# Blocks 2 to 5 of a fused state-space and feed-forward kernel: transposing DMAs, two pairs per feed-forward matmul, tokens on partitions

## The chip, the cores and the metric

The kernel runs on one core of a Trainium2 chip. The time is device microseconds of one execution, and the kernel is judged by the median of its runs. A profile is one further execution, with its own time; its span runs from the first to the last instruction.

## The reference

A state-space layer over 4 batches, 8 heads, 768 tokens, head size 32 and state size 16, then a bilinear feed-forward over the 3072 tokens x 256 features.

```
for c in range(nc):                       # chunks of 32 tokens
    cum = np.cumsum(la, axis=-1)          # la = log(a) of the chunk
    L = np.exp(cum[:, :, :, None] - cum[:, :, None, :]) * causal
    M = np.einsum('bhin,bhjn->bhij', Cc, Bc) * L
    y_intra = np.einsum('bhij,bhjd->bhid', M, xc)
    y_inter = np.einsum('bhin,bhnd->bhid', Cc, state) * np.exp(cum)[:, :, :, None]
    y[:, :, sl] = y_intra + y_inter
    Bx = np.einsum('bhjn,bhjd->bhjnd', Bc, xc) * decay_from_j[:, :, :, None, None]
    state = decay_full[:, :, None, None] * state + np.sum(Bx, axis=2)
x = attn_out.transpose(0, 2, 1, 3).reshape(B * S, H * D)
return (x @ w_a) * (x @ w_b) @ w_out      # w_a, w_b: 256 x 1536, w_out: 1536 x 256
```

## The kernel before

The sequence is cut in 6 blocks of 128 tokens. A *pair* is one block of two batches, so there are 12 pairs; pair p is block p // 2. The decay inside a block is folded into B and C: `scan` makes running products of a, `factors_mm` spreads them to the tokens on TensorE, and `scale_bc` multiplies B and C by the factors (fB, fC) on GpSimd, so that the scores only need a causal mask.

For each pair: six loads (`load1`, L122) bring B, C and x of the two batches, batch bt on partitions 64 bt to 64 bt + 63, two neighbouring tokens on each partition, so that a run in memory is two tokens of a head (128 B for B and C, 256 B for x). `transposes` (L267) turns B and C on TensorE into the PSUM tile SC0; ScalarE evacuates B twice, each time with every second head zeroed, and C once (L274, L275). `scores` (L288) is 32 matmuls on 32 x 64 tiles of the array, into the four PSUM banks SC0 and SC1. `mask` (L321) multiplies each bank by the causal mask on VectorE, or through a ScalarE copy on GpSimd (L319). `pv` then adds the state product (L364), the product of the masked scores with x (L330) and, with `ds_mm` (L347), the sums for the next state; ScalarE writes the result as X2T (L378). `state_sums` (L405, VectorE) and `state_spread` (L412 and L419, GpSimd) make the next block's state as a full 128-column block-diagonal tile per batch.

The feed-forward of a pair has 256 token columns. A *unit* (`unit`, six per pair) is four matmuls for x @ w_a (L432, aps), four for x @ w_b (bps), one ScalarE copy of aps to asb (L444) and one VectorE product hk = bps x asb (L451). `out_half` is 12 matmuls with w_out for 128 tokens (L464), a ScalarE evacuation (L479) and a store (L481). All of these share four PSUM banks in turn (pool `psf`).

The order on every engine is written out by hand. From pair 3 on a loop issues: scores of p, scaling of pair p + 1 on GpSimd, loads of pair p + 2 on the SP queue, masks mixed with units of pair p - 1, output of p - 2, `pv(p)`, the transposes of p + 1. Stores and loads stand on the SP queue in this order too. Weights are loaded and cast by GpSimd's DMA queue, in halves for w_a and w_b and thirds for w_out; `warmup` matmuls run in the first 13 us.

## Time and profile before

| what | value |
|---|---|
| three runs | 131.08, 132.76, 135.22 us (median 132.76) |
| profiled execution | 130.84 us, span 129.1 us |
| TensorE busy | 122.9 us (95%), granted clock 1.0 |
| VectorE, ScalarE, GpSimd busy | 86.5, 75.2, 54.5 us |
| chain that ended last | TensorE 88% |
| feed-forward matmuls | 288 each of aps, bps and ops |
| DMA | 12.22 MB, 43333 packets |

In the rows, a line number is that of the kernel; "out<-in" names tiles; "x32" is a count; for a group, "busy, mean ns" and the idle time before it follow the bar. PEld is TensorE's weight load, which overlaps its matmuls. A matmul's length includes its way through the array, so the cost of one in a row of them is the difference of starts. SPq rows are DMA issues of the SP queue.

### The profile page before, as it was taken

The page shows a single profiled execution, that of the slowest core. Times are in us where ns is not written, and L with a number is a line of the kernel's source. Part 1 is how long each engine was busy: PE and PEld are TensorE (multiplying, and loading weights), DVE is VectorE, ACT ScalarE, POOL GpSimd, SP SyncE. Part 2 cuts the span into 40 slices and gives each one's busy share as a digit, 9 for nine tenths or more (in the row PEclk, how much of TensorE's full clock was granted, in tenths as well). Part 3 has the DMA queues.
Part 4 walks back from the last instruction along what each step waited for, and adds up shares of the span by engine and source line. Part 5 has one row for each costly group of instructions (what it writes and reads, how often), then busy time and mean ns, then how long its engine had stood idle before and what let it go on. Part 6 is the DMA issues. An engine that isn't in the chain of part 4 may idle for free.

```text
span 129.1 us, 4719 instructions
## 1 busy us (share of the span) xinstructions
PE 122.9 (95%) x1944; PEld 101.7 (79%) x1944; DVE 86.5 (67%) x162; ACT 75.2 (58%) x155; POOL 54.5 (42%) x77
## 2 busy tenths in 40 slices
PE   6999989998999999999999999999999999999990
PEld 2254778886888888888888888898888888888880
DVE  1695498693874975956957938948939929734441
ACT  3164946956566476476576576575486485455520
POOL 6777596587809309219129039047056000000000
PEclk9999999999999999999999999999999999999999
DMA  3999999956463542623623434515510110110112
GB/s 68 179 138 227 163 221 186 189 105 122 111 115 115 84 124 64 122 63 74 116 61 86 84 85 96 107 46 106 122 39 28 45 41 5 41 41 5 41 41 81
DMA packets 43333, 12.22 MB, mean 95 GB/s; under 512 B 37552, under 2 KB 43216, under 8 KB 43312
## 3 DMA queue, kind: packets, MB, share of 16 engines
q1 hardware_dynamic: 38256, 8.84, 32.6%
q0 software_dynamic: 2800, 2.63, 13.1%
q10 hardware_dynamic: 2256, 0.46, 1.8%
q8 instruction: 15, 0.25, 0.8%
q14 instruction: 6, 0.05, 0.1%
HBM read 11.13 MB, written 3.15 MB: 111 GB/s over the span
## 4 chain that ended last, share of the span: by engine, by line
PE 88%; DMA 3%; POOL 2%; DVE 2%; ACT 1%; issue 1%; SPq 0%
PE aps L432 25%; PE ops L464 24%; PE bps L432 23%; PE SC L288 3%; PE SC L330 3%; PE SC L267 3%; DMA bn<-in_B_dram 3%; PE SC L364 2%; PE tc L195 1%; DVE t L321 1%; PE fps L219 1%; PE SC L347 1%; POOL xn L122 1%; PE py L330 1%; POOL Wa L136 1%; ACT bt L274 1%
## 5 line engine op out<-in xcount | busy, mean ns | idle before, releaser
L451 DVE TENSOR_TENSOR hk<-bps,asb 128x512 f16<-128x512 f32 x72 | 49.3, 688 | 24.4 <-ACT asb L444 21.9
L444 ACT COPY asb<-aps 128x512 f32<-128x512 f32 x72 | 42.0, 587 | 18.3 <-PE aps L432 16.8
L432 PE MATMUL aps<-X2T,Wa 128*128 128x256 f16 x288 | 43.3, 275 | 0.0
L432 PE MATMUL bps<-X2T,Wb 128*128 128x256 f16 x288 | 42.9, 273 | 0.0
L464 PE MATMUL ops<-Wo,hk 128*128 128x256 f16 x288 | 35.2, 273 | 0.0
L321 DVE TENSOR_TENSOR t<-SC,causal 128x512 f16<-128x512 f32 x45 | 29.5, 682 | 2.8 <-PE SC L288 1.9
L432 PEld LDWEIGHTS <-Wa 128*128 128x128 f16 x288 | 27.5, 99 | 4.4 <-DVE Pr L200 0.3
L432 PEld LDWEIGHTS <-Wb 128*128 128x128 f16 x288 | 28.1, 98 | 3.3
L464 PEld LDWEIGHTS <-hk 128*128 128x128 f16 x288 | 27.7, 98 | 3.1
L412 POOL TENSOR_TENSOR sbd<-U,maskbd 128x512 f16<-128x512 f32 x10 | 11.6, 1160 | 35.7 <-DVE U L405 35.7
L479 ACT ACTIVATE osb<-ops 128x256 f32<-128x256 f32 x23 | 8.7, 386 | 15.7 <-PE ops L464 15.7
L243 POOL TENSOR_SCALAR x<-xn 128x512 f16<-128x512 f32 x9 | 13.4, 1491 | 0.9 <-DMA xn<-in_x_dram 0.2
L378 ACT ACTIVATE X2T<-SC 128x512 f16<-128x512 f32 x11 | 6.6, 597 | 8.3 <-PE SC L347 7.4
L274 ACT ACTIVATE bt<-SC,ch 128x256 f16<-128x256 f16 x22 | 9.2, 472 | 0.4 <-PE SC L267 0.3
L405 DVE SCALAR_TENSOR_TENSOR U<-SC,G,gU 128x64 f32<-128x64 f32 x16 | 3.8, 279 | 5.4 <-ACT X2T L378 5.4
L249 POOL TENSOR_TENSOR bm<-bn,fB 128x256 f16<-128x256 f32 x11 | 6.9, 626 | 0.8 <-DMA bn<-in_B_dram 0.8
L249 POOL TENSOR_TENSOR cm<-cn,fC 128x256 f16<-128x256 f32 x10 | 6.2, 623 | 1.3 <-DMA cn<-in_C_dram 1.3
L288 PEld LDWEIGHTS <-bt 32*64 32x64 f16 x384 | 3.6, 108 | 3.5 <-issue 2.2
L288 PE MATMUL SC<-ct,bt 32*64 32x128 f16 x384 | 5.4, 227 | 0.7 <-ACT ct L275 0.6
L195 PE MATMUL SC<-warm 128*128 128x512 f16 x10 | 4.8, 629 | 1.2 <-DVE warm L159 1.2
L330 PEld LDWEIGHTS <-x 64*32 64x32 f16 x384 | 3.1, 91 | 3.2 <-issue 1.1
L330 PE MATMUL SC<-t,x 64*32 64x128 f16 x352 | 4.6, 218 | 0.7 <-DVE t L321 0.7
(62 smaller groups left out, 73.1 us busy)
## 6 DMA issues: line engine op xcount, KB each, us to landing
out_dram<-osb SPq DMA_DIRECT2D x23, 128.0 KB, 1.7
xn<-in_x_dram SPq DMA_DIRECT2D x21, 128.0 KB, 3.2
bn<-in_B_dram SPq DMA_DIRECT2D x24, 64.0 KB, 3.2
cn<-in_C_dram SPq DMA_DIRECT2D x21, 64.0 KB, 2.9
Wa<-in_moe_w_a_dram POOLq DMA_DIRECT2D x2, 384.0 KB, 5.9
Wb<-in_moe_w_b_dram POOLq DMA_DIRECT2D x2, 384.0 KB, 7.4
Wo<-in_moe_w_out_dram POOLq DMA_DIRECT2D x3, 256.0 KB, 7.4
xn<-in_x_dram POOLq DMA_DIRECT2D x2, 128.0 KB, 7.2
```

Source lines behind the costliest of these rows:

```text
L243: eng.tensor_scalar(xo, xi, XS, None, ALU.mult)
L249: eng.tensor_tensor(out=m_, in0=pair_in[p][which].rearrange("p h r n -> p r h n"), in1=f[:, blk, :, bp].unsqueeze(3).broadcast_to((128, 2, ...
L274: nc.scalar.activation(out=o_, in_=TB, func=AF.Copy, scale=par[:, e : e + 1])
L288: nc.tensor.matmul(SC[m][64 * bt : 64 * bt + 64, c0 : c0 + Q], BT[rows, e, r, bt], CT[rows, bt], start=True, stop=True, skip_group_check=True,
L321: nc.vector.tensor_tensor(out=o_, in0=i_, in1=c_, op=ALU.mult)
L330: nc.tensor.matmul(py[bt][32 * g : 32 * g + 32, u * Q : (u + 1) * Q], s["X16"][k, h, r, :], s["T1"][k, h, r, :], start=(first and u == 0 a ...
L412: nc.gpsimd.tensor_tensor(out=Sbd.rearrange("p t (m c) -> p t m c", m=4), in0=U32[:, p].unsqueeze(2).broadcast_to((128, 2, 4, 2 * D)), in1 ...
L432: nc.tensor.matmul(ps[:, kk * 2 * Q : (kk + 1) * 2 * Q], W[:, f, k * 128 : (k + 1) * 128], X2T[:, p, f].rearrange("p t q -> p (t q)"), sta ...
L444: nc.scalar.copy(asb, a_ps)
L451: nc.vector.tensor_tensor(out=s["hk"][:, 2 * k2 : 2 * k2 + 2, :].rearrange("p k q -> p (k q)"), in0=b_ps, in1=asb, op=ALU.mult)
L464: nc.tensor.matmul(o_ps[:, 0:d_model], hk[:, k, bt * Q : (bt + 1) * Q], Wo[:, k, :], start=(k == 0), stop=(k == NK - 1), skip_group_check= ...
L479: nc.scalar.activation(out=o_sb, in_=o_ps[:, 0:d_model], func=AF.Copy, scale=1.0 / (YS * YS))
```

## The change

From block 2 on (pairs 4 to 11, `P0 = 4`) the layout is another one. Each partition holds one token, and both batches lie side by side on it (`by_token`); B, C and x of a pair come in one load each, with runs of one token (64 B for B and C, 128 B for x). `scale_bc` writes C, and in two copies B, into a tile of six planes of 128 columns, four of them B with every second head zero; `turn` transposes the six planes with one DMA on the SP queue, in place of the transposes on TensorE and their evacuations. Scores become 16 matmuls of 32 x 128 tiles, the product with x 16 of 128 x 32 and the state sums 8; the state product is 8 matmuls of 32 x 64 with a state tile of 64 columns (`spair`), a fraction of the former spread. `outputs` does all this for the two pairs of a block together and writes XB, on whose 512 token columns `bunit` runs the feed-forward, two matmuls for each weight matrix and 128 rows of it; `bout` makes the output of 128 tokens. The four PSUM banks (ff0 to ff3) are taken in a written order (`BANKS`) and no longer in turn. w_out is loaded in two parts with three neighbouring rows on a partition, and the columns of w_a and w_b are read with a step of three to match.

Pairs 0 to 3 keep their layout. In the start, the first loads, warm-ups, scans and masks stand in another order, pair 0's C is cut over two queues, three loads of pair 1 and all of pair 2 go through GpSimd's queue, and C of pair 0 is scaled from PSUM. The written order after pair 2 is new; pair 0's stores stand ahead of pair 4's x on the SP queue.

```diff
+    Wa = [big.tile([128, 2, KC], f16, name=f"Wa{t}") for t in range(2)]
+    Wb = [big.tile([128, 2, KC], f16, name=f"Wb{t}") for t in range(2)]
...
+    X2T = big.tile([128, P0, 2, 2, Q], f16, name="X2T")
+    XB = big.tile([128, NBLK - P0 // NBP, 2, 2, NBP, Q], f16, name="XB")
...
+    planes = [big.tile([128, 6, H * N], f16, name=f"planes{t}") for t in range(2)]
+    causal_q = big.tile([128, Q], f16, name="causal_q")
...
+    hkb = ctx.enter_context(tc.tile_pool(name="hkb", bufs=2))
...
+    def bank(name):
+        return psf.tile([128, 512], f32, name=name, tag=f"ff{next(banks)}")
...
+    def by_token(t_):
+        return t_.rearrange("p h r n -> p (h r n)").rearrange("p (t h n) -> p t h n", t=2, h=H)
...
+    def load2(eng, p, which):
...
+        blk, bp = divmod(p, NBP)
+        return eng.dma_start(
+            by_token(pair_in[p][which]).rearrange("p t h n -> p (t h) n"),
+            (B, C, x)[which][2 * bp : 2 * bp + 2, :, blk * Q : (blk + 1) * Q, :].rearrange("t h q n -> q (t h) n"),
+        )
...
+    def load_wo(half):
+        nc.gpsimd.dma_start(
+            Wo[:, 6 * half : 6 * half + 6].rearrange("p (g kk) e -> p g (kk e)", kk=3),
+            moe_w_out.rearrange("(g p kk) e -> p g (kk e)", p=128, kk=3)[:, 2 * half : 2 * half + 2],
+        )
...
+    load1(nc.scalar, 0, 0, 1)
+    load1(nc.sync, 0, 0, 0)
     load1(nc.scalar, 0, 1, 1)
-    b0 = load1(nc.sync, 0, 0, 0)
-    load1(nc.scalar, 0, 1, 0)
-    load1(nc.sync, 0, 0, 1)
+    load1(nc.sync, 0, 1, 0, 0, 32)
+    nc.sync.dma_start(ch, ph_t.ap())
+    load1(nc.scalar, 0, 1, 0, 32, 32)
     nc.scalar.preload_act_table_set("natural_log_exp_and_others")
     load1(nc.scalar, 0, 2, 1)
     load1(nc.sync, 0, 2, 0)
-    load1(nc.scalar, 1, 1, 1)
     load1(nc.sync, 1, 0, 0)
-    load1(nc.sync, 1, 1, 0)
...
-    w0 = load_w(0)
-    tc.add_manual_dep(w0[0].ins, b0.ins.name, AFTER, reason="first inputs ahead of weights")
+    load1(nc.gpsimd, 1, 0, 1)
+    load1(nc.gpsimd, 1, 1, 0)
+    load1(nc.gpsimd, 1, 1, 1)
+    load_w(0)
     for bt in range(2):
         load1(nc.gpsimd, 1, 2, bt)
-    b2 = load1(nc.sync, 2, 0, 0)
-    tc.add_manual_dep(b2.ins, w0[0].ins.name, AFTER, reason="first weights ahead of pair 2")
-    load1(nc.sync, 2, 0, 1)
-    for w in (1, 2):
-        for bt in range(2):
-            load1(nc.sync, 2, w, bt)
...
+        raw = by_token(pair_in[p][which]) if p >= P0 else pair_in[p][which].rearrange("p h r n -> p r h n")
+        if p >= P0 and which:
+            eng.tensor_tensor(
+                out=planes[p % 2][:, 4:6].rearrange("p t (h n) -> p t h n", n=N),
+                in0=raw,
+                in1=f[:, blk, :, bp].unsqueeze(3).broadcast_to((128, 2, H, N)),
+                op=ALU.mult,
+            )
+            return
...
+        if p >= P0:
+            dst = planes[p % 2][:, 0:4].rearrange("p (t e) (m f n) -> p t e m f n", e=2, f=2, n=N)
+            for e in range(2):
+                eng.tensor_copy(dst[:, :, e, :, e], m_.rearrange("p t (m f) n -> p t m f n", f=2)[:, :, :, e])
...
+    def turn(p):
+        T_ = mid.tile([128, 6, 128], f16, name="turned", tag="turned")
+        nc.sync.dma_start(T_, planes[p % 2].rearrange("p a c -> p (a c)"), transpose=True)
+        st[p]["BT"] = T_[:, 0:4].rearrange("p (t e) k -> p e t k", e=2)
+        st[p]["CT"] = T_[:, 4:6]
...
-        for e in range(2):
+        st[p]["T1"] = mid.tile([128, H, 2, Q], f16, name="t1", tag="t1")
+        for e, bt, m in itertools.product(range(2), range(2), range(4)) if p >= P0 else ():
+            rows = slice(32 * m, 32 * m + 32)
+            c0 = (e * 2 + bt) * Q
+            nc.tensor.matmul(
+                SC[m][:, c0 : c0 + Q],
+                BT[rows, e, bt],
+                CT[rows, bt],
+                start=True,
+                stop=True,
+                skip_group_check=True,
+                tile_position=(32 * m, 0),
+            )
+        for e in range(2) if p < P0 else ():
...
-        for r in range(2):
+        for bt, g in itertools.product(range(2), range(4)) if p >= P0 else ():
+            c0 = 32 * (g ^ 2 * bt)
+            nc.tensor.matmul(
+                py[bt, u][c0 : c0 + 32],
+                by_token(s["X16"])[:, bt, u * 4 + g],
+                s["T1"][:, u * 4 + g, bt],
+                start=False,
+                stop=True,
+                skip_group_check=True,
+                tile_position=(0, c0),
+            )
...
+        for bt, m in itertools.product(range(2), range(4)) if p >= P0 else ():
+            nc.tensor.matmul(
+                s["DS"][bt][32 * m : 32 * m + 32, :],
+                s["bm"][:, bt, 2 * m : 2 * m + 2, :].rearrange("p h n -> p (h n)"),
+                by_token(s["X16"])[:, bt, 2 * m : 2 * m + 2].rearrange("p h d -> p (h d)"),
+                start=True,
+                stop=True,
+                skip_group_check=True,
+                tile_position=(0, 32 * m),
...
+    def outputs(blk):
+        pairs = range(blk * NBP, (blk + 1) * NBP)
+        SCt = (SC0, SC1)
+        cols = [slice(j * Q, (j + 1) * Q) for j in range(NBP)]
+        for j, p in enumerate(pairs):
+            s = st[p]
+            for m in range(4):
+                for bt in range(2):
+                    rows = slice(32 * m, 32 * m + 32)
+                    half = 64 * ((m + bt) % 2)
+                    nc.tensor.matmul(
+                        SCt[bt][half : half + 64, m // 2, cols[j]],
+                        s["Sbd"][rows, bt],
+                        s["CT"][rows, bt],
+                        start=(j == 0),
+                        stop=False,
+                        skip_group_check=True,
+                        tile_position=(32 * m, half),
+                    )
...
+        for j, p in enumerate(pairs):
+            py = {(bt, u): SCt[bt][:, u, cols[j]] for bt in range(2) for u in range(2)}
+            for u in range(2):
+                pv_u(p, u, py, False)
...
+            nc.scalar.activation(
+                out=XB[to, blk - P0 // NBP, :, bt].rearrange("p u j q -> p u (j q)"),
+                in_=SCt[bt][fr, :, 0 : NBP * Q],
+                func=AF.Copy,
+                scale=YS / XS,
...
+        else:
+            Sbd = mid.tile([128, 2, 2 * D], f16, name="spair", tag="spair")
+            nc.gpsimd.tensor_tensor(
+                out=Sbd.rearrange("p t (e d) -> p t e d", e=2),
+                in0=U32[:, p].rearrange("p t (e d) -> p t e d", e=2),
+                in1=par.unsqueeze(1).unsqueeze(3).broadcast_to((128, 2, 2, D)),
+                op=ALU.mult,
+            )
...
                     ps[:, kk * 2 * Q : (kk + 1) * 2 * Q],
-                    W[:, f, k * 128 : (k + 1) * 128],
-                    X2T[:, p, f].rearrange("p t q -> p (t q)"),
+                    W[k // 6][:, f, k % 6 // 3 * 384 : (k % 6 // 3 + 1) * 384].rearrange("p (c kk) -> p kk c", kk=3)[
+                        :, k % 3
+                    ],
+                    X2T[:, p, :, f],
...
+    def bunit(blk, k):
+        s = st.setdefault(("FF", blk), {})
+        if "hk" not in s:
+            s["hk"] = hkb.tile([128, NK, 2 * NBP * Q], f16, name="hkb", tag="hkb")
+        ps = []
+        for W in (Wa, Wb):
+            t_ = bank("aps" if W is Wa else "bps")
+            for f in range(2):
+                nc.tensor.matmul(
+                    t_,
+                    W[k // 6][:, f, k % 6 // 3 * 384 : (k % 6 // 3 + 1) * 384].rearrange("p (c kk) -> p kk c", kk=3)[
+                        :, k % 3
+                    ],
+                    XB[:, blk - P0 // NBP, f].rearrange("p t j q -> p (t j q)"),
+                    start=(f == 0),
+                    stop=(f == 1),
+                    skip_group_check=True,
+                )
+            ps.append(t_)
+        asb = evac_a(ps[0])
+        return lambda: nc.vector.tensor_tensor(out=s["hk"][:, k], in0=ps[1], in1=asb, op=ALU.mult)
...
+    def bout(blk, c, parts=1):
+        bt, j = divmod(c, NBP)
+        hk = st[("FF", blk)]["hk"]
+        rows = out[(2 * j + bt) * S + blk * Q :][0:Q]
+        w = d_model // parts
+        for part in range(parts):
+            o_ps = bank("ops")
...
     warmup(6, SC[3])
+    warmup(2, SC[3], 128)
     scan(0, 1)
     over_mid(0, 1)
     sel_over_mid(0, 1, nc.vector)
+    scan(1, 3)
     v = factors_mm(0, 1)
     nc.vector.reciprocal(flat(fB, 0, 1), v)
+    warmup(2, SC[3])
+    warmup(1, SC[3], 128)
+    scale_bc(0, 0, nc.vector)
+    scale_bc(0, 1, nc.vector, v.rearrange("p (r b h) -> p r b h", r=2, b=NBP)[:, :, 0])
+    tb, tcp = bank("tb"), bank("tc")
+    transposes(0, [tb, tcp], lambda: warmup(1, SC[3], 128))
     nc.scalar.copy(flat(fC, 0, 1), v)
...
+    warmup(5, tcp)
...
+    scan(4, 5)
+    w1 = load_w(1)
+    for bt in range(2):
+        load1(nc.gpsimd, 2, 0, bt)
+    warmup(1, tcp, 128)
...
+    sel_over_mid(1, NBLK, nc.vector)
+    warmup(2, tcp)
+    aps = [unit_mm(0, 0, Wa), unit_mm(0, 1, Wa)]
+    asb = [evac_a(aps[0])]
     scores(1)
+    mask(product(1, 3), by_pool=True)
+    aps.append(unit_mm(0, 2, Wa))
+    asb.append(evac_a(aps[1]))
+    asb.append(evac_a(aps[2]))
+    fps = bank("fps")
+    factors(1, 3, fps)
+    scale_x(1, nc.scalar)
+    for m in range(3):
+        mask(product(1, m))
+    bps = [unit_mm(0, k2, Wb) for k2 in range(3)]
+    for bt in range(2):
+        load1(nc.gpsimd, 2, 1, bt)
+    load_wo(0)
...
+    load_wo(1)
+    tiles(3)
+    for bt in range(2):
+        load1(nc.gpsimd, 2, 2, bt)
+    times(0, 0, bps[0], asb[0])
+    pv(1, DS=(0, SC[:2]), split=True)
+    ds_mm(0, 64, SC[:2])
+    for k2 in range(1, 3):
         times(0, k2, bps[k2], asb[k2])
-    pv(1, then=lambda: ds_mm(0, 320))
-    v = factors_mm(3, NBLK)
+    fb(1)
+    scale_bc(2, 0, nc.gpsimd)
+    scale_bc(2, 1, nc.gpsimd)
+    go((1, 0), (1, 1), (1, 2))
...
+    for t_ in planes:
...
+    b3 = [load1(nc.sync, 3, 0, bt) for bt in range(2)]
+    tc.add_manual_dep(b3[0].ins, w1[1].ins.name, AFTER, reason="weights ahead of pair 3's inputs")
+    for bt in range(2):
+        load1(nc.sync, 3, 1, bt)
+    loads_x(3, nc.sync)
+    loads_bc(4)
+    go((0, 3), (0, 4), (1, 3), (0, 5))
+    transposes(2, apart=True)
...
+    loads_bc(5)
     o = [bank("ops"), bank("ops")]
-    for bt in range(2):
-        out_mm(0, bt, o[bt], range(8))
+    out_mm(0, 0, o[0], range(6))
+    out_mm(0, 1, o[1], range(6))
+    out_mm(0, 0, o[0], range(6, NK))
+    stores = [out_store(0, 0, o[0])]
     pull(2)
-    pv(2)
-    state(2)
+    pv(2, split=True)
+    out_mm(0, 1, o[1], range(6, NK))
+    stores.append(out_store(0, 1, o[1]))
+    h = unit(2, 0, lambda: transposes(3, apart=True))
+    state_sums(2)
...
+    def prep(p, spread=()):
+        if p < NP:
+            scale_bc(p, 1, nc.gpsimd)
+            scale_bc(p, 0, nc.gpsimd)
+            turn(p)
...
+    scores(3)
+    prep(4, (2,))
+    for f in stores:
+        f()
+    loads_x(4, nc.sync)
+    loads_x(5)
+    prep(5)
+    tiles(6)
+    load2(nc.sync, 6, 1)
+    load2(nc.sync, 6, 0)
+    loads_bc(7)
+    mask(product(3, 0))
+    h()
+    for m in range(1, 4):
+        mask(product(3, m))
+    out_half(1, 0)
+    out_half(1, 1)
+    go((2, 2))
+    pull(3)
+    pv(3)
+    state_sums(3)
+    fb(3)
+    state_spread(3)
+    prep_x(4)
+    go((2, 3), (2, 4), (2, 5))
+    out_half(2, 0)
+    o_ps = bank("ops")
+    out_mm(2, 1, o_ps, range(6))
...
+    scores(4)
+    mask(product(4, 3), by_pool=True, by_token=True)
+    scale_x(5, nc.scalar)
+    prep(6)
+    masked(4, (0, 1))
+    out_mm(2, 1, o_ps, range(6, NK))
+    out_store(2, 1, o_ps)()
+    masked(4, (2,), *pu(3, 0))
+    go((3, 1))
+    scores(5)
+    mask(product(5, 3), by_pool=True, by_token=True)
+    mask(product(5, 2), by_pool=True, by_token=True)
+    loads_x(6, nc.sync)
+    prep(7)
+    loads_x(7, nc.sync)
+    loads_bc(8)
+    masked(5, (0, 1), *pu(3, 2, 3, 4, 5))
+    group(2)
+    out_half(3, 0)
+    out_half(3, 1)
...
+    stage(6, True, (4, 5))
+    loads_x(8)
+    prep_x(7)
+    masked(6, (0, 1))
+    masked(6, (2,), *bu(2, 0, 1, 2))
+    scale_x(6, nc.scalar)
+    bgo(2, 3, 4)
+    stage(7, True)
+    loads_bc(9)
+    prep(8)
+    prep(9)
+    loads_x(9, nc.sync)
+    loads_bc(10)
+    masked(7, (0, 1, 2), *bu(2, 5, 6, 7, 8, 9, 10, 11))
+    group(3)
+    bout(2, 0)
+    bout(2, 1)
+    stage(8, True, (6, 7))
+    prep_x(8)
+    prep_x(9)
+    prep(10)
+    loads_bc(11)
+    loads_x(10, nc.sync)
+    masked(8, (0, 1))
+    masked(8, (2,), *bu(3, 0, 1, 2, 3, 4, 5))
...
+    for blk in range(4, NBLK):
+        pB = blk * NBP + 1
+        stage(pB, False)
+        if blk > 4:
+            prep_x(pB)
+        loads_x(pB + 2, nc.sync)
+        prep(pB + 2)
+        masked(pB, (0, 1))
+        bout(blk - 2, 2)
+        masked(pB, (2, 3), *bu(blk - 1, 6, 7, 8, 9))
+        group(blk)
+        bout(blk - 2, 3)
+        bgo(blk - 1, 10, 11)
+        if blk + 1 < NBLK:
+            stage(pB + 1, False, (pB - 1, pB))
+            prep_x(pB + 1)
+            masked(pB + 1, (0, 1))
+            bout(blk - 1, 0)
+            masked(pB + 1, (2,))
+            bout(blk - 1, 1)
+            masked(pB + 1, (3,), *bu(blk, 0, 1, 2, 3, 4, 5))
+    last = NBLK - 1
+    bout(last - 1, 0)
+    bout(last - 1, 1)
+    bgo(last, *range(6))
+    bout(last - 1, 2)
+    bgo(last, *range(6, NK))
+    bout(last - 1, 3)
+    for c in range(3):
+        bout(last, c)
+    bout(last, 3, 2)
```

## The prediction

> **What bounds the kernel now.** I read the busy shares first, then the chain of waits that ended last, then the timeline of TensorE over one pair, and last the rows of the engines that the change loads more.
>
> ```profile
> PE 122.9 (95%) x1944; PEld 101.7 (79%) x1944; DVE 86.5 (67%) x162; ACT 75.2 (58%) x155; POOL 54.5 (42%) x77
> PE 88%; DMA 3%; POOL 2%; DVE 2%; ACT 1%; issue 1%; SPq 0%
> ```
>
> The first line gives the busy time of each engine, the second the shares of the chain. TensorE (PE) is both the busiest and 88% of the chain, so a microsecond taken off its stream is a microsecond off the span as long as nothing else comes forward. The windows show how near the others are in the steady part (busy us of PE, PEld, DVE, ACT, POOL, then granted clock, DMA share, GB/s):
>
> ```profile
> 60.00:70.00 10.00, 10.00 (x167) 8.69 (x168) 7.70 (x15) 5.93 (x13) 4.70 (x7) 1.00 0.42 89
> 70.00:80.00 10.00, 10.00 (x168) 8.70 (x166) 7.44 (x14) 6.42 (x13) 4.79 (x6) 1.00 0.39 84
> ```
>
> TensorE never idles there, VectorE (DVE) is at 0.75, the clock is full. The timeline of one pair (start, length, row) says what the period is made of:
>
> ```profile
> 59.56 0.43 PE L288 MATMUL SC<-ct,bt 32*64 32x128 f16 x32
> 59.92 0.61 PE L432 MATMUL aps<-X2T,Wa 128*128 128x256 f16 x4
> 60.37 0.60 PE L432 MATMUL bps<-X2T,Wb 128*128 128x256 f16 x4
> ...
> 62.55 1.47 PE L464 MATMUL ops<-Wo,hk 128*128 128x256 f16 x12
> 63.86 0.60 PE L432 MATMUL aps<-X2T,Wa 128*128 128x256 f16 x4
> ...
> 64.73 0.39 PE L364 MATMUL SC<-ct,sbd 128*128 128x128 f16 x4
> 65.05 0.42 PE L330 MATMUL SC<-t,x 64*32 64x128 f16 x32
> 65.30 0.32 PE L347 MATMUL SC<-x,bm 64*32 64x64 f16 x16
> 65.56 0.29 PE L267 MATMUL SC<-ident,bm 128*128 128x128 f16 x2
> 65.68 0.28 PE L267 MATMUL SC<-ident,cm 128*128 128x128 f16 x2
> 65.79 1.47 PE L464 MATMUL ops<-Wo,hk 128*128 128x256 f16 x12
> ...
> 68.94 0.43 PE L288 MATMUL SC<-ct,bt 32*64 32x128 f16 x32
> ```
>
> Differences of starts are what counts, since ends overlap. The period is 68.94 - 59.56 = 9.38 us. Twelve output matmuls take 63.86 - 62.55 = 1.31, so 0.1092 us each; 72 feed-forward matmuls make 7.86. The attention part is the rest, 1.52: state product 0.32 (64.73 to 65.05), intra product 0.25, state sums 0.26, transposes 0.23, scores about 0.45 with the turn into and out of their tiling. So the feed-forward is near a floor that the change can't lower much, and 1.5 us of each pair is open to it.
>
> **The change, part by part: feed-forward of blocks 2 to 5.** Two pairs share one 512-column matmul, so the 96 matmuls of a block (two pairs, W_a and W_b) become 48 over the same columns. Price of a 512-column matmul: at most 2 x 109.2 = 218.4 ns; at least the 256-column one plus 256 columns at the slope between two rows of the page. L364's four of 128 columns are 57 ns apart ((390 - 219)/3), L432's four of 256 are 109 apart, so 0.404 ns a column, 212 ns. With 24 per pair the gain is 0 to 0.15 us; I take 0.07. Output matmuls stay at 256 columns.
>
> **Attention matmuls of pairs 4 to 11.** Tokens lie 128 to a block on partitions, no longer even and odd in halves. Transposes leave TensorE: -0.23. Scores fall from 32 matmuls on eighths of the array to 16 on quarters: at least four at a time by the 57 ns row (0.23), at most as before (0.45); I take 0.33. Intra product, 32 to 16, four at a time: 0.23 to 0.25, I take 0.24. State sums, 16 to 8: half of 0.26. State product, 4 full matmuls to 8 on eighths: 8 at the scores' 14 ns is 0.11, at most 0.32; I take 0.13. Sum 0.83 against 1.52: 0.69 less, bounds 0.36 to 0.82 by the ends named. Eight pairs: 8 x (0.69 + 0.07) = 6.1 us.
>
> **ScalarE and GpSimd.** ScalarE loses the three evacuations of the transposes (2 x 472 + 455 ns a pair) and gains some mask copies; it goes from 0.6 busy to less. GpSimd loses two thirds of the state spread (1160 ns for 512 columns, now 128: by the 406 ns row of the same size), gains two small copies a pair (at most 433 ns by the maskbd row) and some masks at 1.16. It has half its time free in the windows, so I cost this at nothing; if the cover were gone, a pair's copies would be 0.9 us. Early it is fuller: 3.6 to 4.1 of each 5 us until 35. Six loads of pair 2 at 0.72 move there, 4.3 us. What is late then is the first turn (pair 4), needed some 9 us after pair 3's scores; by my list of GpSimd's queue it has about 4 us left.
>
> **Start and end.** Three of pair 1's loads go onto GpSimd's queue ahead of the weights (3 x 0.72), a wait of 0.83 for pair 0's B and the 0.77 issue of ch leave it: weights leave 0.6 later and land at about 11.5, the first use was at 12.37. Covered by 0.9 us. The new order of warm-ups, scans and masks, and C cut over two queues, I bound by ±1.5 us (idle of 0.43 and 0.67 us in the timeline near 14 and 16 could go; the first loads end the wait at 4.6 either way) and take -0.4. The last store splits in halves of 128 columns: 24 x 57 ns against 12 x 109, no difference; the tail after the last matmul (some 3.2 us) stays.
>
> **Loads, turns and the SP queue.** This is the part the old trace can't show. Issues on SP (min/median/max ns):
>
> ```profile
> L122 SPq DMA_DIRECT2D bn<-in_B_dram x24: 596/627/1582, 1.2 to 87.6; - x24
> L122 SPq DMA_DIRECT2D xn<-in_x_dram x21: 595/633/1931, 2.7 to 90.5; - x21
> L481 SPq DMA_DIRECT2D out_dram<-osb x23: 332/338/577, 31.6 to 126.4; - x23
> ```
>
> B and x cost the same though x is twice the bytes; both have 512 runs, the store 128. So an issue goes by runs: 0.338 + 0.75 ns for each run above 128. A whole-pair load of the new kind has 2048 runs: 1.78 us (at least 0.63 if it didn't go by runs, at most 4 x 0.63 = 2.5). Runs double, 6144 a pair. The engines' side:
>
> ```profile
> q1 hardware_dynamic: 38256, 8.84, 32.6%
> ```
>
> 32.6% of 16 engines over 129.1 us is 17.6 ns a packet, for pieces of 231 B on average. 6144 pieces of 64 and 128 B cost between half of that and all of it: 3.4 to 6.8 us of 16 engines per pair, under a period of 8.6. The Trainium skill (DMA: Bandwidth & Descriptors, Specifications) speaks against the change here: it puts the smallest transfer for full line rate at 512 B, and its section on small descriptors counts a fixed three cycles for each packet. By it a 128 B piece is 7 cycles and a 64 B piece 5, so halving the pieces would cost 10/7 of the former packet time, an estimate from that page of about 5 us a pair; inside my ends.
>
> A turn (six blocks of 128 x 128, 192 KB) has no row. If it went by 256-byte rows it would be 768 runs, 0.82 us of SP; if by 16-element runs, 6144, 4.85 us. I take 0.8, being nearest to x's runs in length. The same skill page (Latency and other measured facts) gives a transposing DMA 261 GB/s, an estimate of 0.75 us for 192 KB; nothing here shows it.
>
> Does SP keep up? It starts pair 3's six loads when the second weights have landed (12.17 + 7.4, 19.6), is through at 23.4, and then issues 22 whole loads, 8 turns, 10 stores before the last turn is out: 39.2 + 6.4 + 3.4 = 49.0, so 72.4, landed at 75.5. TensorE wants that turn for pair 11's scores, after which it has 108 x 0.109 + 18 x 0.87 + 24 x 0.057 + 0.6 = 29.4 us and the tail of 3.2: 32.6 before the end, at about 91. There is 15 us of room on average, less for the first turns (pairs 5 to 8), where SP's queue holds a turn behind up to four loads (7.1 us). A turn waits for GpSimd's planes, and stores and loads of later pairs queue behind it. I put 0.5 us of stalls on that.
>
> **VectorE.**
>
> ```profile
> L451 DVE TENSOR_TENSOR hk<-bps,asb 128x512 f16<-128x512 f32 x72 | 49.3, 688 | 24.4 <-ACT asb L444 21.9
> L321 DVE TENSOR_TENSOR t<-SC,causal 128x512 f16<-128x512 f32 x45 | 29.5, 682 | 2.8 <-PE SC L288 1.9
> ```
>
> A block asks 12 x 0.688 + 8 x 0.682 + 4 x 0.28 + 0.34 = 15.2 us of it, TensorE 2 x 8.6 = 17.2: 0.88 against 0.80 before. Ahead of a joint group 4 masks and 4 products (5.5 us) stand against 12 output matmuls and 4 units (4.8 us): up to 0.7 late, and TensorE then waits for a bank. I take 0.15 for each of four blocks, 0.6 in all; ends 0 and 2.8.
>
> **The sum.** Span 129.1 - 6.1 - 0.4 + 0.5 + 0.6 = 123.7. Around the span lay 130.84 - 129.1 = 1.74 us, so 125.4 against the profiled 130.84, a ratio of 0.959. The three runs were 131.08, 132.76 and 135.22; the profiled one is under the lowest. Scaled to the median it would be 127.2, to the lowest 125.7; I give 126.2.
>
> **Rivals.**
> First, more gain: attention at its lower ends (0.82 + 0.15 a pair, 7.8), start -1.5, no stalls: span 119.8, time 121.5. For it: VectorE's longest waits are for ScalarE, which gets lighter. Against: every end must hold at once.
>
> Second, VectorE takes the place: 0.6 lost in each of the eight pairs' stages (the 0.7 above is the worst of them), 4.8 less the 0.6 already counted. Span 127.9, time 129.6. For it: 0.88 busy and groups in bursts. Against: units are as long as before (0.87) and four banks sufficed.
>
> Third, slower: the turns hold the SP queue. If a turn keeps SP busy for 4.85 us, SP is through at 23.4 + 39.2 + 38.8 + 3.4 = 104.8, landed 107.8, and with 32.6 behind it the span is 140.4, time 142. It becomes the bound from 2.7 us a turn, and the kernel gets slower than before from 3.5 (23.4 + 39.2 + 28 + 3.4 + 3 + 32.6 = 129.6). For it: no row of a turn, and SP has 1.78 a load to bear. Against: loads run two pairs ahead.
>
> Fourth, the sixteen-matmul forms don't overlap four at a time: scores and intra product 16 x 57 ns each, 0.91, sums and state product 0.46 each: 2.74 against 1.52, 9.8 more for eight pairs, less 0.6 of the feed-forward: span 138.3, time 140. Against: L288 and L330 overlap by eight now.
>
> **How the numbers follow.** Forecast 0.60, first rival 0.10, second 0.15, third 0.11, fourth 0.04. Time 126.2; range 121.5 (first rival) to 131.0 (past the second), leaving out the third and fourth and little of the rest. A measurement of this kernel tells about 2% from no change, so faster means under 130.1. Faster: 0.60 + 0.10 + 0.11 of the second = 0.81. Within 2%: 0.04 of the second, 0.03 of mild cases of the third, 0.01 of the fourth: 0.08. Slower: 0.08 + 0.03 = 0.11.
>
> **What would show it.** Right: scores, intra product, sums and state product together at 0.8 us a pair by starts, 512-column matmuls 212 to 218 ns apart, whole loads of 1.8 us on SP, turns under 2, scores of pairs 5 to 8 waiting for a turn by less than 1 us together, VectorE idle left in each block. Wrong: scores waiting for turned tiles from pair 6 on, SP without gaps, DMA share near 1, or matmuls of the sixteen forms 50 ns apart.

## The result and the profile after

The changed kernel takes 125.9 us (median of six runs, 125.24 to 128.84), the kernel before 132.52 (six runs, 131.08 to 135.22): a ratio of 0.955, 95% interval 0.946 to 0.963. The ratios here are of undisturbed runs alone, since a few runs of either kernel are some per cent longer. The forecast was 126.2. The profiled execution took 125.89 us with a span of 124.2; before it was 130.84 and 129.1, so 4.9 us came off the span and 5.4 had been forecast. The total came out near the forecast. Its terms are less so: the start gave more than forecast, pairs 4 to 11 gave less, and the reckoning of the SP queue was wrong although the stall it led to was small.

The busy times and the shares of the chain, from the page after:

```profile
PE 117.6 (95%) x1471; PEld 79.9 (64%) x1471; DVE 85.4 (69%) x162; ACT 71.6 (58%) x142; POOL 64.2 (52%) x109
PE 63%; DMA 17%; POOL 7%; SPq 7%; issue 3%; DVE 1%; ACT 1%; POOLq 0%; ACTq 0%; DVEq 0%
```

TensorE lost 5.3 busy us and is still 95% of the span, but only 63% of the chain, where it had 88%. Transfers, GpSimd and SP's issues now lie on it with 31% together; some 7 of these 31 points are the first 11.6 us, where the chain runs through pair 0's loads and the first weights. An engine can be busy all the time and a second chain can run just as long beside it; that is the thing to see in these two lines, and the experiments below come back to it. In the windows (busy us of PE, PEld, DVE, ACT, POOL, then granted clock, DMA share, GB/s) after:

```profile
50.00:60.00 10.00, 10.00 (x86) 5.64 (x85) 7.70 (x16) 8.06 (x15) 6.60 (x12) 1.00 1.04 140
60.00:70.00 10.00, 9.84 (x131) 5.88 (x130) 7.60 (x16) 6.66 (x13) 5.23 (x10) 1.00 0.70 97
```

The DMA share went from about 0.4 to 0.7 and 1.04 (it adds up the packets' times, so it can pass 1). TensorE, which never idled in these windows, now does (9.84). The timeline of TensorE over the second joint group (start, length, row), which answers to that of one pair before:

```profile
63.16 0.59 PE L666 MATMUL aps<-XB,Wa 128*128 128x512 f16 x2
63.59 0.59 PE L666 MATMUL bps<-XB,Wb 128*128 128x512 f16 x2
64.12 0.32 PE L507 MATMUL SC<-turned,spair 32*64 32x128 f16 x16
64.36 0.63 PE L418 MATMUL SC<-t,x 128*32 128x128 f16 x32
64.82 0.29 PE L446 MATMUL SC<-x,bm 128*32 128x64 f16 x16
65.04 2.79 PE L693 MATMUL ops<-Wo,hkb 128*128 128x256 f16 x24
68.00 0.40 PE L357 MATMUL SC<-turned 32*128 32x128 f16 x16 [0.16 <-DMA turned<-planes]
68.33 0.61 PE L666 MATMUL aps<-XB,Wa 128*128 128x512 f16 x2
```

Differences of starts, for two pairs: state product 0.24, intra product 0.46, sums 0.22; scores 0.33 for one. So by their own rows the four take 0.12 + 0.23 + 0.11 + 0.33 = 0.79 us a pair, and 0.83 had been forecast. Two 512-column matmuls are 0.43 apart, 216 ns each, in the range of 212 to 218. The row of 63.59 shows what these rows leave out: its two matmuls are followed only after 0.53. The other 0.10 is spent ahead of a change from the whole array to tiles. Every scores row and every joint group pays it, three times for two pairs, so 0.15 us a pair.

### The profile page after: what moved, and what is told of

It reads as the page before. It is cut to its first block, busy times and chain, and to the rows that moved or that the text cites. A ratio compares the mean times of both kernels' runs of the same rounds, so it can differ in the third digit from the quotient of the medians.

```text
span 124.2 us, 3750 instructions
## 1 busy us (share of the span) xinstructions
PE 117.6 (95%) x1471; PEld 79.9 (64%) x1471; DVE 85.4 (69%) x162; ACT 71.6 (58%) x142; POOL 64.2 (52%) x109
## 3 DMA queue, kind: packets, MB, share of 16 engines
q1 hardware_dynamic: 60528, 9.27, 48.8%
## 4 chain that ended last, share of the span: by engine, by line
PE 63%; DMA 17%; POOL 7%; SPq 7%; issue 3%; DVE 1%; ACT 1%; POOLq 0%; ACTq 0%; DVEq 0%
PE ops L693 15%; PE aps L666 13%; PE bps L666 13%; DMA bn<-in_B_dram 8%; PE aps L600 6%; PE bps L600 5%; DMA Wa<-in_moe_w_a_dram 5%; PE ops L636 4%; SPq L347 4%; DMA turned<-planes 3%; SPq L156 3%; POOL bm L303 1%; PE SC L357 1%; POOL cn L147 1%; PE SC L432 1%
## 5 line engine op out<-in xcount | busy, mean ns | idle before, releaser
L678 DVE TENSOR_TENSOR hkb<-bps,asb 128x512 f16<-128x512 f32 x48 | 32.3, 687 | 12.9 <-ACT asb L614 11.8
L666 PE MATMUL aps<-XB,Wa 128*128 128x512 f16 x96 | 28.6, 379 | 0.0
L666 PE MATMUL bps<-XB,Wb 128*128 128x512 f16 x96 | 28.5, 379 | 0.0
L693 PE MATMUL ops<-Wo,hkb 128*128 128x256 f16 (+1 forms) x204 | 22.5, 267 | 0.0
L621 DVE TENSOR_TENSOR hk<-bps,asb 128x512 f16<-128x512 f32 x24 | 16.1, 683 | 3.5 <-ACT asb L614 3.1
L600 PE MATMUL aps<-X2T,Wa 128*128 128x256 f16 x96 | 14.3, 274 | 1.0 <-DMA Wa<-in_moe_w_a_dram 0.7
L600 PE MATMUL bps<-X2T,Wb 128*128 128x256 f16 x96 | 14.1, 273 | 0.0
L636 PE MATMUL ops<-Wo,hk 128*128 128x256 f16 x96 | 11.6, 273 | 0.0
L636 PEld LDWEIGHTS <-hk 128*128 128x128 f16 x96 | 8.9, 98 | 1.5 <-DVE hk L621 0.2
L412 DVE TENSOR_TENSOR t<-SC,causal 128x512 f16<-128x512 f32 x13 | 8.2, 682 | 1.8 <-PE SC L372 1.7
```

The lines of the kernel that those rows point to most:

```text
L412: nc.vector.tensor_tensor(out=o_, in0=i_, in1=c_, op=ALU.mult)
L600: nc.tensor.matmul(ps[:, kk * 2 * Q : (kk + 1) * 2 * Q], W[k // 6][:, f, k % 6 // 3 * 384 : (k % 6 // 3 + 1) * 384].rearrange("p (c kk) -> ...
L621: nc.vector.tensor_tensor(out=s["hk"][:, 2 * k2 : 2 * k2 + 2, :].rearrange("p k q -> p (k q)"), in0=b_ps, in1=asb, op=ALU.mult)
L636: nc.tensor.matmul(o_ps[:, 0:d_model], hk[:, k, bt * Q : (bt + 1) * Q], Wo[:, k, :], start=(k == 0), stop=(k == NK - 1), skip_group_check= ...
L666: nc.tensor.matmul(t_, W[k // 6][:, f, k % 6 // 3 * 384 : (k % 6 // 3 + 1) * 384].rearrange("p (c kk) -> p kk c", kk=3)[:, k % 3], XB[:, b ...
L678: return lambda: nc.vector.tensor_tensor(out=s["hk"][:, k], in0=ps[1], in1=asb, op=ALU.mult)
```

## The experiments

Times are medians in us, the ratio is to the kernel before on the same chip, the span is that of the profiled execution.

| kernel | time | ratio (95%) | span |
|---|---|---|---|
| changed kernel | 125.9 | 0.955 (0.946 to 0.963) | 124.2 |
| changed kernel, again | 125.13 | 0.957 (0.949 to 0.966) | 123.7 |
| new start alone | 129.96 | 0.994 (0.991 to 0.998) | 128.2 |
| units of 256 columns | 126.01 | 0.964 (0.957 to 0.972) | 123.7 |
| scores of 32 matmuls | 126.17 | 0.967 (0.957 to 0.977) | 125.7 |
| four transposes back | 126.45 | 0.968 (0.961 to 0.976) | 124.6 |
| one turn | 125.18 | 0.957 (0.949 to 0.964) | 123.2 |
| two turns a pair | 131.62 | 1.005 (1.000 to 1.010) | 129.8 |
| few loads | 124.65 | 0.953 (0.945 to 0.960) | 122.7 |
| one mask on VectorE | 125.12 | 0.956 (0.949 to 0.963) | 123.0 |
| the same, again | 125.10 | 0.958 (0.951 to 0.965) | 123.2 |
| six masks on VectorE | 127.29 | 0.974 (0.966 to 0.982) | 125.3 |
| six masks, two turns | 132.38 | 1.012 (1.000 to 1.025) | 130.5 |

Most intervals are nearly 1% to each side, so for differences of a few tenths the spans and timelines decide, and "the rest" below is the time from pair 3's scores to the end of the span: 92.3 us in the changed kernel's first profile (31.91 to 124.2), 92.0 in its second.

**The new start alone.** The old layout and the old loop for all pairs, behind the new start and order up to pair 3:

```diff
-    P0 = 4
+    P0 = NP
...
+    for p in range(3, NP):
+        scores(p)
+        if p + 1 < NP:
+            scale(p + 1)
+        if p == 3:
+            for f in stores:
+                f()
+        if p + 2 < NP:
+            load(p + 2)
...
```

> The start and the order up to pair 3's scores are the changed kernel's, but all twelve pairs keep the old layout, TensorE transposes, 256-column units and the loop of the kernel before. Theory: the gain has two separate parts, 1.2 us from the start (pair 3's scores came with two more units behind them) and the rest, some 3.7 us, from pairs 4 to 11. Then the span is about 129.1 - 1.2 = 127.9 us, ratio 0.99. Rival (the start is only shuffled work, and its lead is given back when the loop reaches its old pace): span 129, ratio 1.00. Second rival (most of the gain is in the start): span under 126, ratio under 0.975.

Measured: span 128.2 against 129.1, so the start is worth 0.9 us. By the ratio it is 0.3 to 1.2. At pair 5's scores this kernel is 1.46 us ahead of the one before (48.71 against 50.17), and half a microsecond of that is lost by the end. The rest of the way, from 128.2 to the changed kernel's 124.2 and 123.7, is the work of pairs 4 to 11: 4.0 to 4.5 us.

**Units of 256 columns.** Each of `bunit`'s matmuls cut in two:

```diff
-            for f in range(2):
+            for half, f in itertools.product(range(2), range(2)):
...
-                    t_,
+                    t_[:, 256 * half : 256 * half + 256],
```

> The changed kernel with every 512-column feed-forward matmul of blocks 2 to 5 cut into two of 256 columns (384 in place of 192, twice the weight loads). Theory: only the fixed part of a matmul is paid twice, 2 x 109.2 - 216 = 2.4 ns each, 192 x 2.4 = 0.5 us: span 124.7, ratio about 0.958. Rival (the wide matmuls are what hides the weight loads with a column step of three, and with 256 columns they show): the pitch of the 256-column matmuls is above 112 ns and the span grows by over 1 us, to 125.5 or more.

Measured: from pair 3's scores on the units took 51.94 us by starts against 51.56 in the changed kernel, +0.38, that is 0.05 a pair. The span, 123.7, is no longer than the changed kernel's own two, since waits elsewhere were shorter in this execution, so the 0.05 is a reading of the timeline and not of the time. So the wide matmul brings what the slope of a column says, and no cost of the weights' columns that are read with a step of three shows.

**Scores of 32 matmuls.** The same products, on 32 x 64 tiles as before:

```diff
-        for e, bt, m in itertools.product(range(2), range(2), range(4)) if p >= P0 else ():
+        for e, bt, m, hh in itertools.product(range(2), range(2), range(4), range(2)) if p >= P0 else ():
...
-                SC[m][:, c0 : c0 + Q],
-                BT[rows, e, bt],
+                SC[m][64 * hh : 64 * hh + 64, c0 : c0 + Q],
+                BT[rows, e, bt, 64 * hh : 64 * hh + 64],
```

> The changed kernel with the scores of pairs 4 to 11 as 32 matmuls on 32 x 64 tiles, as before, in place of 16 on 32 x 128. Theory: what the scores cost is the columns streamed through each quarter of the array, and the same columns pass in both forms, so they take the same 0.33 to 0.36 us a pair and the span stays within 0.3 us of 124.2. Rival (the prediction's step: fewer instructions are cheaper, 0.45 against 0.33): 0.1 us more a pair, span 125.1.

The timeline of TensorE around pair 6's scores in this kernel:

```profile
49.95 0.29 PE L418 MATMUL SC<-t,x 128*32 128x128 f16 x8 [1.22 <-POOL t L410]
...
53.01 0.43 PE L357 MATMUL SC<-turned 32*64 32x128 f16 x32
53.38 0.61 PE L666 MATMUL aps<-XB,Wa 128*128 128x512 f16 x2
```

Scores take 53.38 - 53.01 = 0.37 us, and 0.36 before; with 16 matmuls they take 0.33 or 0.34. So halving their number over the same columns gains 0.03 a pair and 0.2 in all, not the 0.12 that the prediction entered. The profile is 1.5 to 2 us longer than the changed kernel's for another reason: the wait of 1.22 at 49.95 (0.47 there in the changed kernel), one of 0.60 for ScalarE's asb at 58.10 and one of 0.36 for pair 8's turn. It was also the longest of this kernel's four runs (125.72 to 127.44), and why these waits grew in it was not found. The median says only that the kernel isn't much slower.

**Four transposes back.** Four transposes on TensorE ahead of each pair's scores, into a bank that the scores overwrite:

```diff
+        for r in range(4) if p >= P0 else ():
+            nc.tensor.transpose(
+                SC[3].bitcast(f16)[:, r * 128 : (r + 1) * 128],
+                st[p]["bm"][:, r % 2].rearrange("p h n -> p (h n)"),
+                ident,
+            )
```

> The changed kernel with four TensorE transposes of 128 x 128 put back ahead of each pair's scores from pair 4 on, into a scores bank that the scores then overwrite; nothing reads them, the turning DMAs stay. Theory: TensorE sets the time and the transposes were worth what they took there, 0.23 us by starts to 0.33 with the change of tiling, so 8 x 0.23 to 0.33 = 1.8 to 2.6 us come back: span 126.0 to 126.8, ratio about 0.975. Rival (TensorE has slack at the scores, which wait for turned tiles anyway): under 0.6 us.

```profile
64.76 2.79 PE L699 MATMUL ops<-Wo,hkb 128*128 128x256 f16 x24
67.39 0.39 PE L355 MATMUL SC<-ident,bm 128*128 128x128 f16 x4
67.71 0.40 PE L363 MATMUL SC<-turned 32*128 32x128 f16 x16
```

The transposes stand 0.32 before the scores, but 24 output matmuls are followed after 2.63 here and after 2.72 ahead of pair 6's scores in the changed kernel (49.87 to 52.59): the 0.10 for the change of tiling has only moved behind the transposes. Net they cost 0.22 a pair, 1.78 in all, and the prediction had 0.23. The rest is 93.3, 1.0 to 1.3 us longer, not 1.8, and less than the 1.8 to 2.6 that had been expected: the waits for a mask (0.47) and a turn (0.16) of the changed kernel are gone from this profile, since TensorE comes later. Of what the removed transposes gain, half a microsecond or a little more is given back as waits.

**One turn.** Only pair 4 is turned, and its tile serves all pairs:

```diff
+        if p == P0:
+            st["turned"] = big.tile([128, 6, 128], f16, name="turned")
+            nc.sync.dma_start(st["turned"], planes[p % 2].rearrange("p a c -> p (a c)"), transpose=True)
+        T_ = st["turned"]
```

> The changed kernel with one turning DMA in all: pairs 5 to 11 use the turned planes of pair 4, seven DMAs are left out. Theory: the turns land 0 to 2.2 us ahead of the scores that want them, only pair 8's were late (0.16 us), so taking them away gives at most 0.5 us: span 123.7 to 124.2. Rival (the SP queue is what paces the middle, and turns of 1.9 us on it hold loads and stores back): span under 123, DMA waits of GpSimd gone.

Measured: span 123.2, rest 92.1, no more than 0.2 below the changed kernel's 92.3 and 92.0. TensorE itself gained more: from pair 3's scores to the start of its last matmul it takes 88.6 us against 89.2 and 88.9, as no scores wait for a turn and the wait for pair 5's mask is down to 0.30. The stretch behind that matmul is 3.5 us here and 3.1 in the other two, because the last store took 0.4 longer; why was not found. So one turn for each pair costs TensorE 0.3 to 0.6 us. GpSimd's waits for C and B (7.0 and 2.8 us in the changed kernel) are gone, as the rival said, and its waits for x are 4.3 in place of 5.9; little of that reaches TensorE.

**Two turns a pair.** Each turn a second time, into a tile that nobody reads:

```diff
+        spare = mid.tile([128, 6, 128], f16, name="spare", tag="spare")
+        nc.sync.dma_start(spare, planes[p % 2].rearrange("p a c -> p (a c)"), transpose=True)
```

> The changed kernel with each turn issued twice, the second into a tile that nobody reads. One more turn is about 1.9 us of the SP queue a pair. Theory: a pair's own turn goes first, so only what is queued behind it is late, and the leads of 0 to 2.2 us at the scores are eaten in part: one to three scores wait some 1 to 2 us each, span 125 to 128. Rival (the prediction's reckoning of 15 us of room on SP): no change, span 124.2 within 0.4.

Measured: 131.62 us, the rest 98.6, 6.3 to 6.6 longer. With 15 us of room on SP, nothing should have happened; both expectations were too low. The way of the delay, first on SP (from the timeline of this kernel), then on GpSimd, then on TensorE:

```profile
37.28 4.61 SPq L347 DMA_TRANSPOSE turned<-planes  x1
41.95 1.29 SPq L349 DMA_TRANSPOSE spare<-planes  x1
43.29 0.58 SPq L156 DMA_DIRECT2D cn<-in_C_dram  x1
```

```profile
46.41 0.62 POOL L295 TENSOR_TENSOR planes<-cn,fC 128x256 f16<-128x256 f32 x1 [1.15 <-DMA cn<-in_C_dram]
...
49.24 2.26 POOL L412 TENSOR_TENSOR t<-tmp,causal_q 128x512 f16<-128x512 f32 x2
```

```profile
51.55 0.29 PE L420 MATMUL SC<-t,x 128*32 128x128 f16 x8 [3.21 <-POOL t L412]
...
72.22 0.40 PE L359 MATMUL SC<-turned 32*128 32x128 f16 x16 [0.68 <-DMA turned<-planes]
```

Pair 6's C is issued at 43.29 instead of 41.51, 1.8 us later: one spare turn of 1.29, and the rest since pair 5's own turn takes 4.61 to issue and not 4.09. GpSimd, whose work stands in a written order, waits for this load, makes pair 6's planes 1.6 later, and only then the masks of pair 5 (`prep(6)` stands ahead of them). TensorE waits 3.21 us at its last two heads of the intra product, where the changed kernel waited 0.47, and its clock drops: the 24 output matmuls of 2.79 us take 4.46 behind this wait. The window shows it (after the engines' busy times: granted clock, DMA share, GB/s):

```profile
52.20:55.50 3.30, 3.30 (x17) 2.24 (x16) 1.18 (x5) 2.00 (x4) 0.98 (x3) 0.50 0.76 158
```

These two make 4.4 of the 6.3 to 6.6 in this profile; scores that wait for turned tiles, as at 72.22, take most of the others. The drop isn't needed for the result: two of the ten runs show a mean clock of 1.0 and still take 131.15 and 131.24 us, where those at 0.987 take 131.47 to 131.79. A spare turn also loads the DMA engines, and whether its time on SP or its time on the engines counts more was not separated.

**Few loads.** Pairs 6 to 11 aren't loaded, and take the inputs of pairs 4 and 5:

```diff
-        if p < NP:
+        if p < 6:
             tiles(p)
             for w in (1, 0):
                 load2(nc.sync, p, w)
+        elif p < NP:
+            pair_in[p] = pair_in[4 + p % 2]
```

> The changed kernel without the loads of pairs 6 to 11; they use the inputs of pairs 4 and 5. Two thirds of the small-run loads are gone, the turns stay. Theory: loads are covered but for the two waits at 50 and 68 us, so at most 0.6 us comes back: span 123.6 to 124.2; and turns take less time on SP, since their 1.2 to 4.1 us are a full queue and not their own cost (1.2 each then). Rival (small runs load the 16 DMA engines so that stores and turns hold TensorE up): over 1.5 us back, span under 122.7.

Measured: span 122.7, the rest 91.4, 0.6 to 0.9 shorter, at or above the 0.6 expected at most and below the rival's 1.5. No wait of TensorE behind pair 3's scores shows in this profile. The turns of the two kernels, as the tile's groups show them (duration of the issue in ns: minimum, median, maximum; then first and last start in us), first the changed kernel, then this one:

```profile
L347 SPq DMA_TRANSPOSE turned<-planes x8: 1211/1867/4091, 33.6 to 87.1; - x8
```

```profile
L347 SPq DMA_TRANSPOSE turned<-planes x8: 1210/1218/4120, 32.5 to 77.0; - x8
```

A turn by itself holds SP for 1.22 us, and by the same view lands 2.8 us after its issue (median; 3.9 in the changed kernel, 5.6 at most). The median of 1.87 and the later landings are the company of the loads. The last turn starts at 77.0 here and at 87.1 in the changed kernel, where the prediction had it through SP at 72.4.

**One mask on VectorE, and again.** Pair 5's second mask of GpSimd given to VectorE, run on two chips, beside the changed kernel on the second:

```diff
-    mask(product(5, 2), by_pool=True, by_token=True)
...
-    masked(5, (0, 1), *pu(3, 2, 3, 4, 5))
+    masked(5, (2, 0, 1), *pu(3, 2, 3, 4, 5))
```

> The changed kernel with one of pair 5's two GpSimd masks moved to VectorE. In the profile TensorE waits 0.47 us at 49.5 for the second of them. Theory: the wait goes and VectorE, 0.73 busy there, has room: 0.3 to 0.5 us back, span 123.8. Rival (VectorE then holds back the units beside it): same or up to 0.5 longer.

> The version with one of pair 5's GpSimd masks on VectorE, again, beside the changed kernel on the same chip. Its first profile took 91.6 us from pair 3's scores to the end. Theory: the wait of 0.2 to 0.65 us at 49 us is gone for good, 0.3 to 0.7 us less than the changed kernel. Rival (the first profile was only a lucky one): within 0.2 us of it.

> The changed kernel itself, beside the next three on one chip. From pair 3's scores to the end it took 92.3 us in its first profile; run to run the waits near 49 and 68 us come and go, so 91.5 to 92.5 is expected, and a ratio of 0.955.

Measured: the rest 91.6 and 91.7, the changed kernel again 92.0. The wait near 49 us is gone, but the joint group now waits 0.23 for VectorE's mask ahead of it. 125.10 against 125.13 us is no difference, so no version came out that beats the changed kernel.

**Six masks on VectorE.** All masks of GpSimd for pairs 4 to 8:

```diff
-        if by_pool:
+        if by_pool and not by_token:
```

> The changed kernel with all six GpSimd masks of pairs 4 to 8 on VectorE (1.16 us each of GpSimd and 0.59 of ScalarE against 0.68 of VectorE). Theory: VectorE is 0.73 to 0.77 busy between 40 and 70 us, so six more masks are 4.1 us more in 30 and it holds, with small waits for it at the joint groups: within 0.5 us of the changed kernel. Rival (the prediction's second: VectorE takes the place): over 1 us more.

```profile
47.69 0.60 PE L600 MATMUL aps<-X2T,Wa 128*128 128x256 f16 x4 [0.46 <-DVE hk L621]
...
55.95 0.59 PE L666 MATMUL aps<-XB,Wa 128*128 128x512 f16 x2 [0.52 <-DVE hkb L678]
```

Measured: the rest 93.8, 1.8 longer, where at most 0.5 had been expected. Three units come 0.6 to 0.7 us late by starts, waiting for VectorE's products to free a PSUM bank of the feed-forward, at 47.69, 55.95 and 72.11; two more, at 60.60 and 62.99, come 0.2 to 0.3 late. The units take 53.74 in all against 51.56. This is the prediction's second rival, in a kernel where its cause exists: with the masks on GpSimd VectorE keeps up, without them it does not.

**Six masks, two turns.** Both edits together, so that GpSimd's masks can't carry the delay:

```diff
-        if by_pool:
+        if by_pool and not by_token:
...
+        nc.sync.dma_start(spare, planes[p % 2].rearrange("p a c -> p (a c)"), transpose=True)
```

> The kernel before this one with each turn issued twice. With GpSimd's masks in place the second turn cost 6.4 us: the SP queue was late, GpSimd waited for x and C (4.4 and 1.2 us), and its masks of pair 5 stood behind that wait; TensorE waited 3.2 us for them and 1 to 2 us each for later tiles. Theory: the way from SP to TensorE led through GpSimd's order, so with no masks there the second turn costs less, the 3.2 us above all: 2 to 3.5 us. Rival (the turned tiles themselves are late by that much): 5.5 to 6.5 us as before.

```profile
44.71 0.40 PE L359 MATMUL SC<-turned 32*128 32x128 f16 x16 [0.95 <-DMA turned<-planes]
...
55.22 0.55 PE L359 MATMUL SC<-turned 32*128 32x128 f16 x16 [2.83 <-DMA turned<-planes]
```

Measured: the rest 99.4, 5.6 longer than with one turn. The way through the masks is closed, and the time is lost all the same, at the scores of pairs 5 and 6, and some 1.6 us more with the slow clock behind the longer wait (granted clock 0.50 from 55.4 to 58.7). The rival was right and the expectation of 2 to 3.5 too low. GpSimd waits 6.06 us for pair 4's x and 1.95 for pair 6's C before it. So the masks are one exit of the delay and the turned tiles another; it arises ahead of both, in the loads.

## Why the prediction was right, and where it was not

**What sets the end.** The prediction said TensorE's stream does, and that 1.5 us of each pair were open to the change. Both held: 0.22 a pair for the transposes and 0.05 for the unit's columns were measured by putting them back, and what is put on TensorE comes out of the span except for what falls into a wait.

**Pairs 4 to 11, forecast 0.76 a pair; measured about 0.62.** The mis-sized term is the attention's 0.83. The forecast summed the rows' own times, which measured 0.79. But the 1.52 of before came from the period of 9.38 less the feed-forward's floor, and that holds the changes of tiling. By the same reckoning after is 0.79 + 0.15, or 0.95 before rounding. So 1.52 - 0.95 = 0.57, and 0.05 for the units. Eight times 0.62 is 5.0 in place of 6.1. The parts: transposes 0.23 (as forecast), state product 0.23 to 0.12 (0.13 forecast), sums 0.26 to 0.11 (0.13), intra product 0.25 to 0.23 (0.24), scores 0.36 to 0.33 (0.33), changes of tiling 0.19 to 0.15 (nothing). Before, one such change stood in the scores' 0.45 and one in the state product's 0.32, as its four matmuls 57 ns apart are 0.23; the forecast's new rows had none. The row is above: 0.53 for two matmuls that are 0.43 apart elsewhere. The Trainium skill (TensorEngine Tiling (Array Packing), Key Properties) says that a change of tiling mode drains TensorE and gives no price; what shows here is 0.10 us ahead of the tiles.

**The start, forecast 0.4; measured 0.9.** Its bound was 1.5 and the choice was low. Within it, one step failed: the weights should have been covered by 0.9 us, and they were not.

```profile
11.59 1.05 PE L600 MATMUL aps<-X2T,Wa 128*128 128x256 f16 x8 [0.73 <-DMA Wa<-in_moe_w_a_dram]
```

They land at 11.5 as forecast, but pair 0 is ready earlier than before, so TensorE waits 0.73 us for them. A moved load has to be held against the new time of its first use, not the old one.

**Stalls, forecast 0.5; measured about 0.8.** The sum is right in kind and wrong in place. Of scores waiting for a turn there is the 0.16 at 68.00. The larger one is at pair 5's intra product, where TensorE waits for a mask of GpSimd. The prediction had put GpSimd's masks at nothing, because it has half its time free:

```profile
49.52 0.29 PE L418 MATMUL SC<-t,x 128*32 128x128 f16 x8 [0.47 <-POOL t L410]
```

A third, 0.14, is a unit at 57.00 waiting for ScalarE's asb.

**VectorE, forecast 0.6; measured about nothing.** The step counted all eight masks of a block on VectorE. Six masks of pairs 4 to 8 are GpSimd's, as the written order has it. The kernel with all masks of pairs 4 to 11 on VectorE is 1.8 us longer, so the danger was real and the change had already dealt with it.

Together: 5.0 - 0.8 is 4.2 for pairs 4 to 11, and the spans say 4.0 to 4.5. With 0.9 from the start it is 5.1 against the 5.4 of the forecast (4.9 by the spans). The errors are -1.1 for pairs 4 to 11, nearly all of it the attention, -0.3 for the stalls, +0.6 for VectorE and +0.5 for the start. The total came out near because they cancel, and that is luck.

**The SP queue: right that it doesn't decide, wrong why.** The forecast had the last turn through SP at 72.4 us; in the profile that is 88.3. The items between are the ones reckoned, 22 loads, 8 turns and 10 stores. They start 3.3 us later (26.7, as pair 3's six loads take 7.2 us and not 3.8), their rows take 51.5 us where 49.0 had been reckoned, and SP waits 10.1 us among them, which had been put at nothing. That the 51.5 is near is luck: loads 26.0 against 39.2, turns 16.0 against 6.4, stores 9.5 against 3.4. One of the waits, from 76.15 to 78.18, on SP's timeline:

```profile
74.42 1.73 SPq L706 DMA_DIRECT2D out_dram<-osb  x2
78.18 1.22 SPq L347 DMA_TRANSPOSE turned<-planes  x1
```

The forecast was 1.78 us for each load of 2048 runs; the group of x's loads in the changed kernel is

```profile
L156 SPq DMA_DIRECT2D xn<-in_x_dram x6: 390/789/1971, 36.7 to 83.8; - x6
```

The same load takes 0.39 us or 1.97. Short ones come behind a turn or a store, long ones behind other loads, but for one of 1.49 right behind a turn: the number of runs alone doesn't set the time. The turn, forecast 0.8, takes 1.22 at its shortest and 2.0 on average. The waits are the step that failed outright: room was counted by adding up SP's own work. A turn waits for GpSimd's planes, these for a load, and that load stands on SP behind an earlier turn and the stores. The chain that ended last shows one round of it (start, length, what):

```profile
38.78 2.67 SPq L347
...
42.13 3.73 DMA bn<-in_B_dram
...
51.91 2.00 SPq L347
...
56.18 6.72 DMA bn<-in_B_dram
63.06 0.62 POOL bm L303
...
64.30 3.65 DMA turned<-planes
```

Turn, transfer of the load behind it, scaling and planes, next turn, and at 68.0 the scores. From landing to use the turned tiles are ahead by 2.2 us for pair 4 (about 4 had been reckoned), 0.1 for pair 6, nothing for pair 8, and 1.3 to 2.0 for the last three pairs, where 15 us had been reckoned. The two-turn kernel measures what that means: one more turn a pair, 1.3 us of SP, takes away the whole gain. The third rival had its bound at 2.7 us a turn and "slower than before" from 3.5; two turns, 2.5 us by their shortest rows, already bring the kernel to 1.005 of before. So the threshold lies between one turn and two, well under the rival's figures; its chance of 0.11 was for a turn of 4.85 us.

Two of the prediction's signs of being wrong came up: SP was almost without gaps from 33.6 to 64.3 us (28.4 of 30.7 us in its rows), and the DMA share was near 1. TensorE all the same lost only about 0.8 us to waits behind pair 3's scores, and 0.6 to 0.9 came back when most loads were left out.

**The other rivals.** More gain (121.5) needed the attention at 0.70 a pair, a start of 1.5 and no stalls; it got 0.95, 0.9 and 0.8. Matmuls that don't overlap (140): 16 scores in 0.33 us are 21 ns apart, so they do.

**The DMA engines.** 6144 pieces a pair had been put at half to all of 17.6 ns each, 3.4 to 6.8 us of 16 engines. The queue's line in the changed kernel, with few loads and with one turn:

```profile
q1 hardware_dynamic: 60528, 9.27, 48.8%
```

```profile
q1 hardware_dynamic: 25440, 6.38, 26.6%
```

```profile
q1 hardware_dynamic: 54928, 7.89, 41.0%
```

48.8% of 16 engines over 124.2 us for 60528 packets is 16.0 ns each, but that is a mean over loads, stores and turns. The 35088 packets that few loads leaves out took 12.8 ns each, so a pair's 6144 pieces are about 4.9 us: inside the range and near the prediction's other estimate of about 5. The 5600 packets of the seven turns took 29 ns each, 1.4 us of 16 engines for each turn, and the prediction counted nothing of the engines for them. Together that is 6.3 us a pair, beside the stores, and two pairs take some 15 us (68.00 to 82.95 between scores), so a DMA share near 1 is in reach wherever loads bunch.

## What to carry to other kernels

Compare like with like when a period is taken apart: if the old cost is "period less floor", it includes changes of tiling and the like, and the new cost must too. The room of a queue isn't the end less its own work; follow the loop through every engine that waits for it (issue, landing, scaling, next issue), and test the room by doubling one item. And fewer matmul instructions over the same columns gain little where they already overlap: what paid here was work that left TensorE altogether, and columns that were halved.
